# Sliding-window attention and a gated feed-forward network on one core: part of the start-up order, the third half's transposes and the last output block are arranged anew

## The chip, the core and the metric

The kernel runs on one core of a Trainium2 chip. The metric is the device time of one execution in microseconds (us). Times of the kernel before are the median of seven runs; a profile is taken of one further execution.

The engines have the profile's names: PE is TensorE (matmul; PEld its weight load), DVE is VectorE, ACT is ScalarE, POOL is GpSimd, SP is SyncE. Each runs its own instructions in the order in which the program gives them and waits for others by semaphores. DMA transfers are issued by SyncE or by GpSimd.

## The reference

```
# q, k, v: (4, 8, 768, 64) float32; n_global = 8, n_local = 96
scores = q @ k^T / 8
keep   = key is one of the first 8 tokens, or 0 <= query - key < 96
dist   = |query - key|, or 96 where a global key is not local
scores = where(keep, scores - slope[h] * dist, -1e9)      # slope[h] = 2^-(h+1)
a      = softmax(scores)
x      = (a @ v), heads put side by side: (3072, 512)
out    = (relu(x @ w_gate) * (x @ w_val)) @ w_out         # 512 -> 1536 -> 512
```

The output is 3072x512 float32.

## The kernel before, in words

**Tiles.** The 3072 queries are taken in eight *halves* of 384 (half s is batch s//2, part s%2 of its 768 tokens), the heads in four *pairs* p. Keys are grouped in seven tiles of 120 local keys and the 8 global ones (128 partitions). For a half and pair, `piece_t(s, p)` (L280) transposes q and k on TensorE into one PSUM bank; `piece_copy` (L294) brings them to SBUF on VectorE: the keys by `put_keys` (L259) in three copies (L270, L271, and L272, a small copy from kT to kT that spreads the global keys), the queries in two (L300), into qT, where each head of a pair has the other's rows at zero (`zero_q`, L194, sets those zeros with two memsets). Half 0 is loaded as float32 in four parts of two heads by SyncE and cast on chip by `piece_cast` (L250), so one transpose takes both heads of a pair (six per pair). Halves 1 and 2 are cast by the load itself (`load_qk_cast`, L117, four transfers on GpSimd's queue) and need one transpose of 64 columns per head (twelve per pair). Halves 3 to 7 are loaded by SyncE, cast by GpSimd (L338, L346) and transposed by DMA.

**Scores.** For half 0 and pairs 0, 1 and 3 of half 1 the distance bias is put into PSUM by matmuls (`piece_bias`, L304, from `sid` and `dd`), then `piece_biased` (L316) adds the products of q and k (L330) in three groups of one bank and takes the exponential of each (L335). Everywhere else `piece_qk` takes the product (L382), the exponential (L385) and multiplies with a mask `m_all[h]` on VectorE (L394). `setup_mask(h)` (L237) makes the eight masks on ScalarE.

**Values and norm.** `piece_av_wide` (L430) makes the denominators (keys' ones) and the value sums of a pair in two banks (L441); `piece_norm_wide` (L448) takes Ln (L451) and Exp (L453) on ScalarE and multiplies on VectorE (L456) into xT[half], a slice per pair. Four slices make the input of the feed-forward network.

**Feed-forward.** `ffn_pieces(c)` (L468) gives, for each of 12 column groups fc, `gate` (four matmuls of 384 columns, L478, one for each slice of xT; Relu on ScalarE, L487) and `val` (four more; multiplication with the Relu on VectorE into ht, L494); and for three row blocks n `outp` (twelve matmuls of 512 columns, L501, a copy on ScalarE, L506, one store of 256 KB by SyncE, L507). The weights come in three groups of four fc (`load_w`, L168: wg0, wv0, ... 512 KB each in bf16 after casting). PSUM has eight banks: three "qk", two "av", three "ff".

**Order.** All engines follow the order of the program text. Halves 0 and 1 are interleaved by hand (L553–L655); after them `weave` places attention pieces between feed-forward pieces by their share of the work (f_items are the backbone, placed items stand at a share of its sum). GpSimd's order is, at the start: the constants of the masks (affine_select), v's globals and tiles 0 to 3 (L138, L151), half 1's k, q, k, q of four heads each (L128), wg0, wv0 (L168), zeroing (L198, L592 to L594), v tiles 4 to 6, weight groups 1 and 2, half 2's k and q, wo; then v of half 2, zeroing for batch 1, v of half 3. Half 2's transposes and copies lie at 0.55 to 0.95 of the first `weave`:

```
T2 = [(0.0, f) for p in range(HP) for f in (lambda p=p: piece_t(2, p, *QKB), lambda p=p: piece_copy(2, p))]
weave(f1_1[G[0]] + f1_0[G[1]][4:] + f1_1[G[1]], ..., spread(T2, 0.55, 0.95))
```

F0 is the list of half 0's gate and val pieces: F0[2*fc] is gate(fc), F0[2*fc+1] is val(fc).

Of the kernel before, what the change touches and what calls it, by code (L numbers as in the profile page):

```python
# [15 lines left out]
def kernel(  # L16
# [12 lines left out]
    nc = tc.nc  # L29
# [43 lines left out]
    gr_pool = ctx.enter_context(tc.tile_pool(name="gr", bufs=3))  # L73
# [31 lines left out]
    def load_qk(s, h0, h1):  # L105
        b, half = divmod(s, 2)
        if s not in qs_of:
            qs_of[s] = stage.tile([128, H, NN * D], FP32, name="qs")
            ks_of[s] = stage.tile([128, H, NN * D], FP32, name="ks")
        for src, dst in ((k, ks_of[s]), (q, qs_of[s])):  # L110
            nc.sync.dma_start(
                out=dst[:, h0:h1, :],
                in_=src[b, h0:h1, half * QH : (half + 1) * QH, :].rearrange(
                    "h (p n) d -> p h (n d)", n=NN))
# [3 lines left out]
    def load_qk_cast(s, parts=2):  # L118

        b, half = divmod(s, 2)  # L120
        n = H // parts
        for i, (src, name) in enumerate(((q, "qs"), (k, "ks"))):
            t = stage.tile([128, H, NN * D], FP32, name=name)
            qk16[s, i] = t.rearrange("p h x -> p (h x)").bitcast(BF16).rearrange(
                "p (h x) -> p h x", h=H)[:, :, 0 : NN * D]
        for h in range(0, H, n):
            for i, src in ((1, k), (0, q)):
                nc.gpsimd.dma_start(  # L128
                    out=qk16[s, i][:, h : h + n],
                    in_=src[b, h : h + n, half * QH : (half + 1) * QH, :].rearrange(  # L130
                        "h (p n) d -> p h (n d)", n=NN))
# [55 lines left out]
    gsrc = setupp.tile([NG, 2, NN, WQ], FP32)  # L187
    gl = setupp.tile([NG, 2, NN, WQ], FP32)
# [32 lines left out]
    nc.gpsimd.affine_select(out=gl[:, 0], in_=gsrc[:, 0], compare_op=ALU.is_ge, fill=BIG,  # L221
# [3 lines left out]
    nc.gpsimd.affine_select(out=gl[:, 1], in_=gsrc[:, 1], compare_op=ALU.is_ge, fill=BIG,  # L225
# [91 lines left out]
    def piece_biased(s, p):  # L317
# [6 lines left out]
        for g, bank in enumerate(banks_of_half[half]):  # L324
            ps = qk_of[s, p][g]
            es = es01[:, g] if g < 2 else es2
            c = 0
            for j, a, w, m in bank:
                n_ = 2 * NN * w
                nc.tensor.matmul(ps[:, c : c + n_], lhsT=kt[:, j, :], rhs=qd[:, :, :, a : a + w],  # L330
                                 start=False, stop=True, skip_group_check=True)
# [138 lines left out]
    def ffn_pieces(c):  # L470
# [11 lines left out]
        def gate(fc, d0=0, d1=N_DC):  # L482
            psg = products(f"g{fc % 2}", wg, fc, d0, d1)
# [77 lines left out]
    load_qk_cast(1)  # L561
    load_w_group(0)
    for h in range(2, 6):
        setup_mask(h)
# [3 lines left out]
    cast(0, 1, V, V)  # L568
    cast(0, 2, A, A)
# [4 lines left out]
    piece_biased(0, 0)  # L574
# [24 lines left out]
    load_qk_cast(2)  # L599
# [3 lines left out]
    def S1(p):  # L603
        if p == 2:
            for g in range(3):
# [29 lines left out]
    AV(1, 2, *QKB)  # L635
    F0[7]()
# [5 lines left out]
    for h in (0, 1, 6, 7):  # L642
        setup_mask(h)
    load_v_half(2)
# [8 lines left out]
    T2 = [(0.0, f) for p in range(HP) for f in (lambda p=p: piece_t(2, p, *QKB), lambda p=p: piece_copy(2, p))]  # L653
# [52 lines left out]
```

The softmax here doesn't subtract the row's maximum and nothing guards it: scores larger than these inputs give would overflow.

## Time and profile before

| | |
|---|---|
| median of 7 runs | 253.21 us (253.14 to 253.85) |
| the profiled execution | 252.88 us |
| its span | 251.1 us |
| busy, share of the span | PE 95%, ACT 62%, DVE 55%, POOL 35% |
| TensorE matmuls | 1741, 239.7 us busy |
| feed-forward products (L478) | 768 of 326 ns |
| output products (L501) | 280 recorded, 379 ns busy each |

The span is the time from the first to the last instruction that the profiler shows; the execution's own time has 1.8 us more around it. The page divides the span into 40 slices of 6.3 us each and gives each engine's busy share in tenths. "Idle before <-X" behind a group of instructions says how long its engine stood idle just before them and who released it. A time in microseconds without further words is a point on the span's axis.

### The profile page before, as it was taken

The page shows a single profiled execution, that of the slowest core. Times are in us where ns is not written, and L with a number is a line of the kernel's source. Part 1 is how long each engine was busy: PE and PEld are TensorE (multiplying, and loading weights), DVE is VectorE, ACT ScalarE, POOL GpSimd, SP SyncE. Part 2 cuts the span into 40 slices and gives each one's busy share as a digit, 9 for nine tenths or more (in the row PEclk, how much of TensorE's full clock was granted, in tenths as well). Part 3 has the DMA queues.
Part 4 walks back from the last instruction along what each step waited for, and adds up shares of the span by engine and source line. Part 5 has one row for each costly group of instructions (what it writes and reads, how often), then busy time and mean ns, then how long its engine had stood idle before and what let it go on. Part 6 is the DMA issues. An engine that isn't in the chain of part 4 may idle for free.

```text
span 251.1 us, 4845 instructions
## 1 busy us (share of the span) xinstructions
PE 239.7 (95%) x1741; PEld 142.5 (57%) x1749; DVE 137.3 (55%) x352; ACT 156.8 (62%) x323; POOL 88.5 (35%) x205
## 2 busy tenths in 40 slices
PE   7678999999999999999999999999999999999993
PEld 4565665556445566556664666556655666556541
DVE  5959557966441467527662557527662557424410
ACT  7886774257654687557774687557774687553321
POOL 8997442059491076203627065303520000000000
PEclk9999999999999999999999999999999999999998
DMA  6999999959599667738468958738432100020012
GB/s 183 174 182 189 206 197 207 138 162 140 83 208 160 197 162 162 53 109 265 106 86 89 252 158 158 56 111 261 104 86 82 43 3 0 19 110 0 0 42 84
DMA packets 77431, 31.56 MB, mean 126 GB/s; under 512 B 57440, under 2 KB 74336, under 8 KB 77408
## 3 DMA queue, kind: packets, MB, share of 16 engines
q0 software_dynamic: 36080, 9.48, 37.0%
q1 hardware_dynamic: 41328, 21.78, 32.0%
q8 instruction: 13, 0.21, 0.4%
q14 instruction: 10, 0.08, 0.1%
HBM read 28.38 MB, written 6.29 MB: 138 GB/s over the span
## 4 chain that ended last, share of the span: by engine, by line
PE 83%; DVE 7%; ACT 6%; DMA 1%; issue 1%; SPq 1%; ACTq 0%
PE ff_ps L478 45%; PE ff_ps L501 24%; PE av_ps L410 5%; PE qk_ps L382 5%; DVE xT L427 2%; DMA qs<-in_q_dram 1%; DVE ht L494 1%; ACT es L335 1%; PE av_ps L441 1%; ACT grelu L487 1%; ACT rcp L424 1%; PE qk_ps L330 1%; ACT lnd L419 1%; DVE qT L300 1%; PE qk_ps L290 1%
## 5 line engine op out<-in xcount | busy, mean ns | idle before, releaser
L478 PE MATMUL ff_ps<-xT,wv 128*128 128x384 bf16 x384 | 78.1, 326 | 0.8 <-DVE ht L494 0.3
L478 PE MATMUL ff_ps<-xT,wg 128*128 128x384 bf16 x384 | 78.1, 326 | 0.0
L487 ACT ACTIVATE grelu<-ff_ps 128x384 bf16<-128x384 f32 x96 | 46.9, 489 | 33.7 <-DVE ht L494 12.5
L501 PE MATMUL ff_ps<-wo_sb,ht 128*128 128x512 bf16 x280 | 66.4, 379 | 0.4
L494 DVE TENSOR_TENSOR ht<-ff_ps,grelu 128x384 bf16<-128x384 f32 x96 | 53.3, 555 | 21.3 <-PE ff_ps L478 13.3
L427 DVE TENSOR_TENSOR xT<-av_ps,rcp 64x384 bf16<-64x384 f32 x48 | 26.7, 555 | 46.2 <-ACT rcp L424 41.6
L478 PEld LDWEIGHTS <-wv 128*128 128x128 bf16 x384 | 36.0, 97 | 23.4 <-issue 2.1
L478 PEld LDWEIGHTS <-wg 128*128 128x128 bf16 x384 | 36.0, 97 | 22.9
L394 DVE TENSOR_TENSOR es<-es,m_all 128x432 bf16<-128x432 bf16 (+5 forms) x113 | 34.4, 333 | 26.1 <-ACT es L385 25.3
L385 ACT ACTIVATE es<-qk_ps 128x432 bf16<-128x432 f32 (+2 forms) x75 | 39.4, 529 | 9.4 <-PE qk_ps L382 7.7
L501 PEld LDWEIGHTS <-ht 128*128 128x128 bf16 x288 | 27.0, 97 | 28.3
L419 ACT ACTIVATE lnd<-av_ps 64x384 f32<-64x384 f32 x48 | 23.3, 485 | 13.3 <-PE av_ps L410 12.6
L506 ACT COPY osb<-ff_ps 128x512 f32<-128x512 f32 x24 | 14.0, 585 | 26.7 <-PE ff_ps L501 25.9
L338 POOL CAST kc<-ks 128x384 bf16<-128x384 f32 x20 | 10.1, 550 | 51.7 <-DMA ks<-in_k_dram 51.7
L382 PE MATMUL qk_ps<-qT,kT 128*128 128x432 bf16 (+5 forms) x113 | 25.8, 286 | 0.0
L151 POOL DMA_DIRECT2D vbuf<-in_v_dram x28 | 24.3, 874 | 4.0 <-DMA wg<-in_moe_w_gate_dram 2.4
L410 PEld LDWEIGHTS <-vbuf 128*128 128x128 bf16 x216 | 18.3, 98 | 8.6 <-issue 0.8
L410 PE MATMUL av_ps<-es,vbuf 128*128 128x216 bf16 (+4 forms) x216 | 21.4, 226 | 0.6 <-DVE xT L427 0.6
L382 PEld LDWEIGHTS <-kT 128*128 128x128 bf16 x113 | 10.9, 98 | 7.5
L424 ACT ACTIVATE rcp<-lnd 128x384 f32<-128x384 f32 x24 | 12.5, 523 | 0.8
L346 POOL CAST qz<-qs 128x192 bf16<-128x192 f32 x40 | 12.2, 353 | 1.4 <-DMA qs<-in_q_dram 1.4
L335 ACT ACTIVATE es<-qk_ps 128x432 bf16<-128x432 f32 (+2 forms) x15 | 7.0, 536 | 3.4 <-PE qk_ps L330 3.3
(92 smaller groups left out, 146.1 us busy)
## 6 DMA issues: line engine op xcount, KB each, us to landing
out_dram<-osb SPq DMA_DIRECT2D x24, 256.0 KB
ks<-in_k_dram SPq DMA_DIRECT2D x5, 768.0 KB
qs<-in_q_dram SPq DMA_DIRECT2D x5, 768.0 KB
vbuf<-in_v_dram POOLq DMA_DIRECT2D x24, 120.0 KB, 4.6
wg<-in_moe_w_gate_dram POOLq DMA_DIRECT2D x3, 512.0 KB, 8.8
wv<-in_moe_w_val_dram POOLq DMA_DIRECT2D x3, 512.0 KB, 10.5
wo_sb<-in_moe_w_out_dram POOLq DMA_DIRECT2D x1, 1536.0 KB, 19.0
ks<-in_k_dram SPq DMA_DIRECT2D x4, 192.0 KB
```

Of the source, the lines that this page charges most:

```text
L151: nc.gpsimd.dma_start(out=v_dst(b, NG + r0, NG + r0 + n, j), in_=v[b, :, KT * j + r0 : KT * j + r0 + n, :].rearrange("h p d -> p h d"))
L382: nc.tensor.matmul(ps[:, c : c + n_], lhsT=kt[:, j, :], rhs=qd[:, :, :, a : a + w], start=True, stop=True)
L385: nc.scalar.activation(es[:, 0:cols], ps[:, 0:cols], AF.Exp, bias=0.0, scale=scale)
L394: nc.vector.tensor_mul(e4, e4, mk)
L410: nc.tensor.matmul(av3[:, :, a : a + w], lhsT=vb[:, j, z0 : z0 + 128], rhs=es[:, c : c + NN * w].rearrange("k (n p) -> k n p", n=NN), star ...
L419: nc.scalar.activation(ln[o0 : o0 + 64], av[d0 : d0 + 64, 0:QH], AF.Ln, bias=0.0, scale=1.0)
L424: nc.scalar.activation(rc, ln, AF.Exp, bias=0.0, scale=-1.0)
L427: nc.vector.tensor_tensor(xT_of[s][r, p, :], av_of[s, p, e_][r, 0:QH], rc[r], op=ALU.mult)
L478: nc.tensor.matmul(st[key][:, 0:QH], lhsT=w_of(w, dc, fc), rhs=xT_of[c][:, dc, :], start=(dc == 0), stop=(dc == N_DC - 1))
L487: nc.scalar.activation(gr, psg[:, 0:QH], AF.Relu, bias=0.0, scale=1.0)
L494: nc.vector.tensor_tensor(ht[:, fc, :], psv[:, 0:QH], st["r", fc], op=ALU.mult)
L501: nc.tensor.matmul(ps2, lhsT=ht[:, fc, n * 128 : (n + 1) * 128], rhs=wo_sb[:, fc, :], start=(fc == 0), stop=(fc == N_FC - 1))
```

## The change

- Half 1's q and k: four transfers as before, but wg0 is issued between the first two and the last two (so wg0 comes earlier in the queue, the last two later).
- Of the masks, only number 4 is made at the start; 5 is made ahead of the scores of half 1's pair 2, and 0, 1, 2, 3, 6, 7 behind F0[11].
- Half 0's cast of pair 1 goes from VectorE to ScalarE; pair 2's q cast is put between the first and second exponential of pair 0's scores (`between`).
- Half 1's first transposes, and their copies, are put among half 0's last scores and norms: t(1,0) ahead of the scores of pair 3, copy(1,0), t(1,1) and copy(1,1) around the second norm. `zero_q` for half 1 now stands behind these copies in the program; the two write the same tile.
- Gates 0 to 2 of half 0 take three of their four slices first, and the last one after the scores of half 1's pair 0. The order of what follows is new too. Four Relu buffers instead of three.
- Half 2's q and k are loaded as float32 (768 KB each, on GpSimd's queue), cast by GpSimd in pairs, and transposed in six transposes a pair; transposes and copies of a pair are one item of `weave`. The loads of v for half 2 stand behind these casts.
- The last block of rows of the last half is computed and stored in columns 0–255, 256–383 and 384–511, the last copied by VectorE.
- Two constants of the masks' set-up are bf16, one of them half as large.

```diff
@@ -105 +105 @@
-    def load_qk(s, h0, h1):
+    def load_qk(s, h0, h1, eng=nc.sync):
...
-    def load_qk_cast(s, parts=2):
...
+    def load_qk_cast(s, h0=0, h1=H):
...
@@ -283,10 +281,10 @@
-                for e in range(1 if s == 0 else 2):
-                    r = slice(0, 128) if s == 0 else slice(64 * e, 64 * e + 64)
-                    src = (cast_of[s, p][:, i, n] if s == 0
-                           else qk16[s, i][:, 2 * p + e, n * D : (n + 1) * D])
+                for e in range(2 if s == 1 else 1):
+                    r = slice(64 * e, 64 * e + 64) if s == 1 else slice(0, 128)
+                    src = (qk16[s, i][:, 2 * p + e, n * D : (n + 1) * D] if s == 1
+                           else cast_of[s, p][:, i, n])
@@ -317 +315 @@
-    def piece_biased(s, p):
+    def piece_biased(s, p, between=None):
@@ -335 +333 @@
+            if g == 0 and between is not None:
+                between()
@@ -482 +482 @@
-            psg = products(f"g{fc % 2}", wg, fc, d0, d1)
+            psg = products(f"g{fc % 4}", wg, fc, d0, d1)
@@ -510,8 +510,24 @@
         for fc in range(N_FC):
             f1.append((0.65, lambda *d, fc=fc: gate(fc, *d)))
             f1.append((0.65, lambda *d, fc=fc: val(fc, *d)))
+        def outp_cols(n, c0, c1, copy):
+            ps2 = ff_psum.tile([128, 512], FP32, name="ff_ps")
+            for fc in range(N_FC):
+                nc.tensor.matmul(ps2[:, 0 : c1 - c0], lhsT=ht[:, fc, n * 128 : (n + 1) * 128],
+                                 rhs=wo_sb[:, fc, c0:c1], start=(fc == 0), stop=(fc == N_FC - 1))
+            if c0 == 0:
+                st["osb"] = osb_pool.tile([128, DM], FP32, name="osb")
+            osb = st["osb"]
+            copy(osb[:, c0:c1], ps2[:, 0 : c1 - c0])
+            nc.sync.dma_start(out=out_v[c, n][:, c0:c1], in_=osb[:, c0:c1])
+
         f2 = []
         for n in range(NN):
+            if c == NHALF - 1 and n == NN - 1:
+                f2.append((1.3, lambda n=n: outp_cols(n, 0, 256, nc.scalar.copy)))
+                f2.append((0.7, lambda n=n: outp_cols(n, 256, 384, nc.scalar.copy)))
+                f2.append((0.7, lambda n=n: outp_cols(n, 384, 512, nc.vector.tensor_copy)))
+                continue
             for part in range(2):
                 f2.append((1.3, lambda n=n, part=part: outp(n, part)))
         return f1, f2
@@ -558,34 +574,39 @@
     load_v_globals(0)
     for j in range(4):
         load_v(0, j)
-    load_qk_cast(1)
-    load_w_group(0)
-    for h in range(2, 6):
-        setup_mask(h)
+    load_qk_cast(1, 0, H // 2)
+    load_w(wg[0], moe_w_gate, 0, GW * 128)
+    load_qk_cast(1, H // 2, H)
+    load_w(wv[0], moe_w_val, 0, GW * 128)
+    setup_mask(4)
     warm_up(7)
     piece_bias(0, 0)
     cast(0, 0, V, V)
-    cast(0, 1, V, V)
-    cast(0, 2, A, A)
+    cast(0, 1, A, A)
+    piece_cast(0, 2, 1, A)
     piece_t(0, 0)
     piece_copy(0, 0)
     piece_bias(0, 1)
     piece_t(0, 1)
-    piece_biased(0, 0)
+    piece_biased(0, 0, lambda: piece_cast(0, 2, 0, A))
     piece_copy(0, 1)
     piece_t(0, 2)
     piece_biased(0, 1)
     piece_copy(0, 2)
     cast(0, 3, V, V)
-    copy_v_globals(V, 0, 1, 4)
     piece_bias(0, 2)
     piece_biased(0, 2)
     piece_t(0, 3)
+    copy_v_globals(V, 0, 1, 4)
+    piece_bias(0, 3)
     piece_copy(0, 3)
-    piece_bias(0, 3)
     AV(0, 0)
+    piece_t(1, 0, *QKB)
     piece_biased(0, 3)
+    piece_copy(1, 0)
     AV(0, 1)
+    piece_t(1, 1, *QKB)
+    piece_copy(1, 1)
 
     zero_q(P, 1)
     for p in range(HP):
@@ -596,52 +617,55 @@
         load_v(0, j)
     load_w_group(1)
     load_w_group(2)
-    load_qk_cast(2)
+    load_qk(2, 0, H, nc.gpsimd)
     load_w(wo_sb, moe_w_out, 0, DM)
 
 
     def S1(p):
         if p == 2:
+            setup_mask(5)
             for g in range(3):
                 piece_qk(1, p, g)
         else:
             piece_bias(1, p)
             piece_biased(1, p)
 
-    piece_t(1, 0, *QKB)
-    AV(0, 2, *QKB)
-    piece_copy(1, 0)
-    piece_t(1, 1, *FFB)
+    def TC(s, p, *pool):
+        piece_t(s, p, *pool)
+        piece_copy(s, p)
+
+    gate, val = F0[0:8:2], F0[1:8:2]
+    AV(0, 2, *FFB)
     AV(0, 3)
-    piece_copy(1, 1)
+    gate[0](0, LAST)
     S1(0)
+    for f in gate[1:3]:
+        f(0, LAST)
+    for f in gate[0:3]:
+        f(LAST, N_DC)
     copy_v_globals(V, 0, 4, NT)
-    piece_t(1, 2, *FFB)
+    S1(1)
+    piece_t(1, 2)
+    piece_t(1, 3)
     piece_copy(1, 2)
-    S1(1)
-    piece_t(1, 3, *FFB)
     piece_copy(1, 3)
-    F0[0]()
+    gate[3]()
     S1(2)
-    F0[1]()
-    F0[2]()
+    val[0]()
+    val[1]()
     AV(1, 0)
-    F0[3]()
     S1(3)
-    F0[4]()
-    F0[5]()
+    val[2]()
     AV(1, 1)
-    F0[6]()
+    val[3]()
     AV(1, 2, *QKB)
-    F0[7]()
     F0[8]()
     AV(1, 3)
     F0[9]()
     F0[10]()
     F0[11]()
-    for h in (0, 1, 6, 7):
+    for h in (0, 1, 2, 3, 6, 7):
         setup_mask(h)
-    load_v_half(2)
     for p in range(HP):
         nc.gpsimd.memset(kT[1][p][:, 3, 32:128].bitcast(mybir.dt.uint32), 0)
         nc.gpsimd.memset(kT[1][p][:, 6, NG + 48 : 128].bitcast(mybir.dt.uint32), 0)
@@ -650,7 +674,10 @@
         nc.gpsimd.memset(qz[i].rearrange("t n p e z -> t (n p e z)").bitcast(mybir.dt.uint32), 0)
     for j in range(NT):
         fill_ones(nc.gpsimd, 1, j)
-    T2 = [(0.0, f) for p in range(HP) for f in (lambda p=p: piece_t(2, p, *QKB), lambda p=p: piece_copy(2, p))]
+    for p in range(HP):
+        cast(2, p, P, P)
+    load_v_half(2)
+    T2 = [(0.0, lambda p=p: TC(2, p, *QKB)) for p in range(HP)]
     weave(f1_1[G[0]] + f1_0[G[1]][4:] + f1_1[G[1]],
           [(0.05 + 0.06 * j, lambda j=j: fill_ones(nc.vector, 0, j)) for j in range(NT)],
           [(0.6, lambda: load_qk_after(3)), (0.6, lambda: load_v_half(3))],
```

More of the change, by code (lines that the diff above doesn't have):

```diff
@@ L72 @@
     ht_pool = ctx.enter_context(tc.tile_pool(name="ht", bufs=2))
-    gr_pool = ctx.enter_context(tc.tile_pool(name="gr", bufs=3))
+    gr_pool = ctx.enter_context(tc.tile_pool(name="gr", bufs=4))
     osb_pool = ctx.enter_context(tc.tile_pool(name="osb", bufs=2))
@@ L110, in load_qk @@
         for src, dst in ((k, ks_of[s]), (q, qs_of[s])):
-            nc.sync.dma_start(
+            eng.dma_start(
                 out=dst[:, h0:h1, :],
@@ L116 @@
     qk16 = {}
-    def load_qk_cast(s, parts=2):
+    def load_qk_cast(s, h0=0, h1=H):
         b, half = divmod(s, 2)
[L121 to L131, printed above, removed]
+        for i, src, name in ((1, k, "ks"), (0, q, "qs")):
+            if (s, i) not in qk16:
+                t = stage.tile([128, H, NN * D], FP32, name=name)
+                qk16[s, i] = t.rearrange("p h x -> p (h x)").bitcast(BF16).rearrange(
+                    "p (h x) -> p h x", h=H)[:, :, 0 : NN * D]
+            nc.gpsimd.dma_start(
+                out=qk16[s, i][:, h0:h1],
+                in_=src[b, h0:h1, half * QH : (half + 1) * QH, :].rearrange(
+                    "h (p n) d -> p h (n d)", n=NN))
     def v_dst(b, r0, r1, j):
@@ L186 @@
         load_qk(0, 2 * p, 2 * p + 2)
-    gsrc = setupp.tile([NG, 2, NN, WQ], FP32)
-    gl = setupp.tile([NG, 2, NN, WQ], FP32)
+    gsrc = setupp.tile([NG, NN, WQ], BF16)
+    gl = setupp.tile([NG, 2, NN, WQ], BF16)
     warm = setupp.tile([128, 128], BF16)
@@ L220 @@
     q1, q2 = [[1, NN], [NN, WQ]], [[0, 2], [-1, NN], [-NN, WQ]]
-    nc.gpsimd.affine_select(out=gl[:, 0], in_=gsrc[:, 0], compare_op=ALU.is_ge, fill=BIG,
+    nc.gpsimd.affine_select(out=gl[:, 0], in_=gsrc, compare_op=ALU.is_ge, fill=BIG,
                             base=-NL, pattern=q1, channel_multiplier=-1)
@@ L224 @@
                             base=0, pattern=q1, channel_multiplier=-1)
-    nc.gpsimd.affine_select(out=gl[:, 1], in_=gsrc[:, 1], compare_op=ALU.is_ge, fill=BIG,
+    nc.gpsimd.affine_select(out=gl[:, 1], in_=gsrc, compare_op=ALU.is_ge, fill=BIG,
                             base=-(NL - 1), pattern=q1, channel_multiplier=0)
```

## The prediction, as put on record before the changed kernel was run

> **What bounds the kernel now.** I read the page's busy line, slices and chain first.
>
> ```profile
> PE 239.7 (95%) x1741; PEld 142.5 (57%) x1749; DVE 137.3 (55%) x352; ACT 156.8 (62%) x323; POOL 88.5 (35%) x205
> ...
> PE   7678999999999999999999999999999999999993
> ...
> PE 83%; DVE 7%; ACT 6%; DMA 1%; issue 1%; SPq 1%; ACTq 0%
> ```
>
> TensorE bounds it: only the first four slices (25 us) and the last have gaps. Windows of the stages that the change touches (columns: sum, then busy time of PE, PEld, DVE, ACT, POOL; clock; DMA share; GB/s):
>
> ```profile
> 13.90:22.90 9.00, 7.49 (x137) 5.76 (x134) 6.29 (x20) 6.44 (x15) 7.92 (x15) 1.00 1.47 186
> 22.90:35.90 13.00, 13.00 (x151) 8.33 (x150) 7.67 (x20) 10.20 (x23) 5.91 (x8) 1.00 1.35 202
> 44.10:52.00 7.90, 7.90 (x85) 4.70 (x85) 7.55 (x27) 1.96 (x4) 0.00 (x0) 1.00 1.29 108
> ```
>
> From 22.9 us TensorE is full; whatever is to be won in front of it is idle time before that. Between 44 and 52 VectorE is nearly full too (7.55 of 7.90) and GpSimd idle. Full speed of the clock (1.00) throughout. The page's own time was 252.88 (span 251.1 and 1.8 around it); the median of seven runs is 253.21, 0.33 above. I add up against 252.88 and put 0.33 on top.
>
> **1. Up to 13.9 us: 0.** Moving the cast (0,1) from VectorE to ScalarE would let the first copy of half 0 start at about 5.8 instead of 6.39. It gains nothing, by the timelines of VectorE and GpSimd:
>
> ```profile
> 6.94 0.26 DVE L272 COPY kT<-kT 128x56 bf16<-128x56 bf16 x1
> ...
> 8.34 0.64 DVE L272 COPY kT<-kT 128x56 bf16<-128x56 bf16 x1
> ...
> 9.98 0.54 DVE L272 COPY kT<-kT 128x56 bf16<-128x56 bf16 x1
> ```
>
> ```profile
> 5.36 3.62 POOL L151 DMA_DIRECT2D vbuf<-in_v_dram  x4
> 8.96 0.80 POOL L128 DMA_DIRECT2D ks<-in_k_dram  x1
> ```
>
> The small SBUF-to-SBUF copy L272 takes 0.18 when GpSimd is quiet (45.32, 47.19, 49.05, 50.92). Here it ends, within 7 ns each time, where an issue of GpSimd ends (7.20, 8.98, 10.52): it waits for the issue in progress. A copy 0.6 earlier comes just behind the issue end at 6.29 and ends at 7.20 again. The bf16 selections on GpSimd: 0; the affine_selects lie on one line by element count whatever their type (216 elements 0.36–0.53, 432 0.58–0.60). Bounds −0.9 (everything one issue of GpSimd earlier) to +0.1.
>
> **2. 13.9 to 35.9: +0.97.** Half 1's k and q of pairs 0 and 1 (cast on load, GpSimd's queue) land at 13.69 and 14.73 in before (q issued 9.73, 5.0 to landing), and stand at the same place in the queue in the changed kernel. Now t(1,0) stands in TensorE's order ahead of qk(0,3), which ran at 14.00, and both wait for q:
>
> ```profile
> 14.00 0.68 PE L330 MATMUL ff_ps<-qT,kT 128*128 128x432 bf16 x4
> ...
> 17.27 0.45 PE L441 MATMUL av_ps<-es,vbuf 128*64 128x216 bf16 x8 [0.42 <-DVE xT L456]
> ...
> 18.20 0.37 PE L312 MATMUL qk_ps<-dd,sid 128*128 128x192 bf16 x4 [0.17 <-DVE xT L456]
> 19.45 0.34 PE L312 MATMUL qk_ps<-dd,sid 128*128 128x216 bf16 x2 [0.87 <-DVE qT L300]
> 19.63 0.75 PE L330 MATMUL qk_ps<-qT,kT 128*128 128x144 bf16 x5
> ```
>
> The columns are start, time, engine, line, operation, and in brackets the idle time before it and its releaser. So qk(0,3) starts at 14.73 and 0.33 (six transposes of q)≈15.08, 1.08 late. Behind it, row by row:
>
> - ScalarE: its exponentials (1.29 for three) end 16.77; then ln and exp of pairs 1, 2, 3 in a chain (0.43+0.50 each): 17.71, 18.63, 19.57.
> - VectorE, in its new order: xT01 (0.56) to 18.30; copy(1,1) to 19.54 (1.32, the sum of L270–L300 without a held L272); xT02 to 20.12; xT03 to 20.60.
> - The partial gate products take three of four k-slices, xT00–02. TensorE reaches them at 18.74; two slices run, the third waits for 20.12. So they cover 0.3 of a gap of 1.4, since copy(1,1) stands before xT02.
> - GpSimd: the zeroing of half 1's qT (L198, 2×0.73), which ran at 13.53, now waits by the changed program's dependences for copy(1,1), 19.54; it ends 21.13. qk(1,0) waits for it: 21.18 instead of 19.63. Behind it in GpSimd's in-order queue: kT and vbuf zeroing, v tiles 4–6, weight groups 1 and 2, k and q of half 2, wo, then the casts.
> - TensorE from there (bias 0.6, qk 0.6, transposes 0.33 and 0.12 for the switch, product 0.65, values 0.28 each): rest of gates 0–2 to 23.24; bias and qk(1,1) 24.44; t(1,2), t(1,3) 25.32; gate 3 25.97; copy(1,2) ends 26.42, so 0.5 of stall, and qk(1,2) starts 26.47; values 0 and 1 of the FFN 28.46; qk(1,3) 30.41; value 3 32.65; last three products to 36.84. Before, the same product F0[11] ended at 35.87.
>
> So +0.97: TensorE's work is the same, and about 3.6 us instead of 2.4 are idle before it is dense. Late loads hold nothing by their rows (issue to landing 8.8 and 10.5 for a weight tile): v 4–6 about 27.9 (needed 28.8), group 1 30.5 and 33.0 (needed 33.4, 34.9). Bounds −0.1 (the partial gates cover all and q lands by 13.9) to +1.5 (v tiles 0.5 later than worked out).
>
> **3. Masks: +0.90.** Of eight exponentials of the bias masks four ran early and four here; now one is early, one ahead of pair 2, and six are here, on ScalarE between two relus:
>
> ```profile
> 35.42 0.49 ACT L487 ACTIVATE grelu<-ff_ps 128x384 bf16<-128x384 f32 x1 [0.67 <-PE ff_ps L478]
> 35.81 1.91 ACT L237 ACTIVATE m_all<-dd 128x432 bf16<-128x432 bf16 x4
> 37.62 0.89 ACT L487 ACTIVATE grelu<-ff_ps 128x384 bf16<-128x384 f32 x2
> ```
>
> ```profile
> 38.15 0.81 PE L478 MATMUL ff_ps<-xT,wv 128*128 128x384 bf16 x4 [0.17 <-ACT grelu L487]
> ```
>
> Four already hold TensorE 0.33 (37.82 to 38.15; three FFN banks are all it may run ahead). Two more, 2×0.453 by their spacing, come wholly on top: no cover is left. Bounds +0.4 (if ScalarE stands a product further ahead) to +0.9.
>
> **4. Half 2's transposes: −0.12.** Twelve half-width transposes per pair cost TensorE 0.55 with their two switches; six full-width ones of casts by GpSimd 0.33: 4×0.22=−0.88. But VectorE had a period of 1.86 there (1.36 copy and 0.5 ht) for 1.86 of TensorE, so TensorE, now at 1.63, waits for it; and GpSimd's issues of v for half 2, queued behind the casts, fall at about 47–54, where it was idle, and hold L272 of pairs 1–3 by 0.2–0.6 (step 1's rows): stalls of about 0.76. Bounds −0.88 to +0.7. k and q, 768 KB each as fp32, land about 40 and 42.4 at the rate of SyncE's load of the same shape (325–365 GB/s), so q's first cast ends at about 43 against a need at 45.87; at the casting queue's 206 GB/s, 45.4, which adds 0.2–0.5. GpSimd's casts: 0.55 each (row L338). The Trainium skill ("SBUF — State Buffer", Who interferes with whom) says that VectorE in its two-port modes and GpSimd lock a shared port pair for a whole instruction. L272 agrees. For this step it would have L272 wait for a running cast of GpSimd as well; by the page, as an estimate, one cast of 0.55 more, 254.6 in all, against 254.05 by the rows; no row of before has L272 beside such a cast.
>
> **5. Last block in columns: −0.9.** After the last product (ends 247.10):
>
> ```profile
> 247.19 0.58 ACT L506 COPY osb<-ff_ps 128x512 f32<-128x512 f32 x1 [2.05 <-PE ff_ps L501]
> ```
>
> Copy to 247.77, SyncE's issue to 248.13, data 248.63–249.44 (0.815 for 256 KB), end 251.1. A 128-column copy on VectorE takes about 0.28 (0.17 for 24, 0.56 for 384): −0.3; the last 64 KB a quarter of 0.815: −0.6. The products are the same (columns add up). Bounds −0.3 (transfer time fixed) to −1.2.
>
> **Sum:** 0+0.97+0.90−0.12−0.90=**+0.85**; 252.88+0.85+0.33≈**254.05**.
>
> **Rivals.** About 0.2% (0.5 us) is what measurement tells from no change. (a) Forecast, 253.75–254.6: chance 0.45. (b) The second half's stages are not held: GpSimd's issues of v end before copy(2,1) or lie between the copies; place the four pairs near 46–52, price the 0.76; +0.09, 253.3, not slower. It decides if fewer than half the L272 there exceed 0.2. For it: four issues of 0.8 in 7.4 us miss some copies; against: all four small copies in the early rows were held. 0.16. (c) k/q of half 2 or casts late, or copies held by casts: +0.6 to +1.3, 254.6–255.3. For: everything on GpSimd's queue starts 6 us later; against: 3 us margin by SyncE's rate. 0.17. (d) The reorder works: q lands by 13.9 or the gates cover the front; term 2 goes to 0, 253.1: 0.12; with (b), 252.3: 0.05. (e) The change doesn't do what it says: the partial gates wait as whole ones (xT03's time), +0.3 more, 254.35: 0.05.
>
> Faster (below 252.7): the joint case 0.05, and with the low bounds of steps 1 and 5 0.05 of (d) and 0.02 of (b): 0.12. Same: 0.14 of (b), 0.07 of (d), 0.04 of (a): 0.25. Slower: 0.41 of (a), (c), (e): 0.63. The range reaches from (b) and (d) at low bounds to (c)'s upper part, 252.6 to 255.2, and leaves out the joint case and (c)'s end.
>
> **What would show it.** Step 2: qk(0,3) at about 15.1, a wait of qk(1,0) for POOL near 21, F0[11] ending about 36.8. Step 3: six masks in a row and a TensorE gap of about 1.2 behind them. Step 4: six transposes a pair, L272 above 0.2 and ending with GpSimd's issues. Step 5: a last copy of 0.28 and about 0.9 less from last product to end. Wrong if qk(0,3) still starts by 14.1, or if masks leave no gap.

## The result, and the profile after

The changed kernel took 254.70 us (median of 14 runs, 253.82 to 255.37) against 253.22 for the kernel before on the same occasions (33 runs): ratio 1.0050, 95% interval 1.0038 to 1.0061. It is slower by about 1.3 to 1.5 us. The forecast was 254.05, range 252.6 to 255.2. The profiled execution took 254.82, its span is 252.8 (before: 252.88 and 251.1).

In what follows t(s,p), copy(s,p) and qk(s,p) are the transposes, the copies and the scores of half s's pair p, and wg1 and wv1 the gate and value weights of the second weight group.

The page after, the same three lines as of before:

```profile
PE 239.1 (95%) x1741; PEld 143.7 (57%) x1749; DVE 134.8 (53%) x351; ACT 157.5 (62%) x326; POOL 91.0 (36%) x211
...
PE   7768988999999999999999999999999999999995
...
PE 75%; DMA 7%; ACT 6%; POOL 4%; DVE 4%; issue 2%; POOLq 0%; ACTq 0%; DVEq 0%
```

TensorE has the same work. But the chain that ended last now runs 7% through DMA (before 1%) and 4% through GpSimd (before none): the start of the program waits for loads. The windows say the same (same columns as before; the second now ends where F0[11] ends, 38.12 instead of 35.87, and the third is half 2's transposes, 3 us later; the columns are sum, then busy time of PE, PEld, DVE, ACT, POOL; clock; DMA share; GB/s):

```profile
13.90:22.90 9.00, 6.65 (x101) 4.77 (x102) 5.40 (x15) 5.25 (x12) 3.07 (x9) 1.00 1.16 168
22.90:38.12 15.22, 13.86 (x179) 8.98 (x178) 8.60 (x24) 11.49 (x26) 13.91 (x28) 1.00 1.10 143
47.10:55.00 7.90, 7.90 (x67) 5.25 (x64) 7.40 (x27) 2.50 (x6) 7.90 (x12) 1.00 1.49 167
```

GpSimd was busy 7.92 in the first window and is now busy 3.07; its work has moved into the second window (13.91 of 15.22). TensorE idles 2.35 in the first window (1.51 before) and 1.36 in the second (0.00 before).

Where the time went is read best by one clock: the start of the n-th feed-forward matmul of 384 columns (L478; four of them make one gate or value product). Each kernel has 768 of these matmuls, all recorded, counted here from 0. Their order is the same in both kernels from the 32nd on.

| matmul | before | after | difference |
|---|---|---|---|
| 0 (first gate slice) | 22.87 | 18.83 | −4.04 |
| 32 (fifth gate) | 32.42 | 33.67 | +1.25 |
| 48 (behind F0[11]) | 35.87 | 38.12 | +2.25 |
| 60 (behind the masks) | 38.15 | 41.30 | +3.15 |
| 92 (ahead of half 2's transposes) | 43.35 | 46.50 | +3.15 |
| 150 (behind them) | 55.54 | 57.79 | +2.25 |
| last product of TensorE ends | 247.10 | 249.69 | +2.59 |
| span ends | 251.1 | 252.8 | +1.7 |

So the front costs 2.25, the masks 0.90, half 2 gives 0.90 back, and the last block 0.88 (from the last product's end to the span's end 4.01 before, 3.13 after). The other 0.34 come in bit by bit between 58 and 247. Of them 0.28 lie ahead of the last feed-forward product, where e4 below, whose program is that of before up to there, shows 0.27 too; so this isn't the change. The remaining 0.06 are in the last block's own products.

TensorE's timeline after, the rows that answer to those shown of before:

```profile
14.89 0.36 PE L288 MATMUL qk_ps<-ident,qs 128*64 128x128 bf16 x6 [0.67 <-DMA qs<-in_q_dram]
15.18 0.69 PE L328 MATMUL ff_ps<-qT,kT 128*128 128x432 bf16 x4
...
20.26 0.32 PE L478 MATMUL ff_ps<-xT,wg 128*128 128x384 bf16 x1 [0.93 <-DVE xT L456]
...
21.25 0.75 PE L328 MATMUL qk_ps<-qT,kT 128*128 128x144 bf16 x5
...
36.16 0.82 PE L478 MATMUL ff_ps<-xT,wv 128*128 128x384 bf16 x4 [0.93 <-DMA wv<-in_moe_w_val_dram]
...
41.30 0.81 PE L478 MATMUL ff_ps<-xT,wv 128*128 128x384 bf16 x4 [1.06 <-ACT grelu L487]
```

Row 1: TensorE waits for q's landing. Row 2: half 0's last scores, at 14.00 before. Row 3: the third slice of the partial gate waits 0.93 for xT02. Row 4: half 1's first scores, at 19.63 before. Row 5: wv1 lands late. Row 6: the masks, which stand in a row on ScalarE:

```profile
38.06 2.81 ACT L235 ACTIVATE m_all<-dd 128x432 bf16<-128x432 bf16 x6
```

GpSimd's timeline has the cause of row 5. Before:

```profile
13.53 1.52 POOL L198 MEMSET qT<- 64x768 uint32 x2
...
18.93 0.80 POOL L168 DMA_DIRECT2D wg<-in_moe_w_gate_dram  x1
```

After:

```profile
12.85 0.78 POOL L166 DMA_DIRECT2D wv<-in_moe_w_val_dram  x1
19.68 1.52 POOL L196 MEMSET qT<- 64x768 uint32 x2 [6.05 <-DVE qT L298]
...
25.30 0.80 POOL L166 DMA_DIRECT2D wg<-in_moe_w_gate_dram  x1
```

The zeroing waits 6.05 us for VectorE's copy, and all later work of GpSimd waits behind it, the loads of v and of the weight groups 1 and 2 among it.

In half 2, two pairs' transposes on TensorE, before (first the keys' six of twelve) and after (six in all):

```profile
44.09 0.36 PE L290 MATMUL qk_ps<-ident,ks 128*64 128x128 bf16 x6
...
45.95 0.36 PE L290 MATMUL qk_ps<-ident,ks 128*64 128x128 bf16 x6
```

```profile
47.15 0.50 PE L288 MATMUL qk_ps<-ident,qk 128*128 128x128 bf16 x6
...
48.78 0.50 PE L288 MATMUL qk_ps<-ident,qk 128*128 128x128 bf16 x6
```

The pairs follow one another at 1.63 instead of 1.86.

### The profile page after: what moved, and what is told of

Its sections match the earlier page's. It is cut to its first block, busy times and chain, and to the rows that moved or that the text cites. A ratio compares the mean times of both kernels' runs of the same rounds, so it can differ in the third digit from the quotient of the medians.

```text
span 252.8 us, 4857 instructions
## 1 busy us (share of the span) xinstructions
PE 239.1 (95%) x1741; PEld 143.7 (57%) x1749; DVE 134.8 (53%) x351; ACT 157.5 (62%) x326; POOL 91.0 (36%) x211
## 4 chain that ended last, share of the span: by engine, by line
PE 75%; DMA 7%; ACT 6%; POOL 4%; DVE 4%; issue 2%; POOLq 0%; ACTq 0%; DVEq 0%
PE ff_ps L478 41%; PE ff_ps L501 23%; PE av_ps L410 5%; PE qk_ps L382 4%; DMA wv<-in_moe_w_val_dram 4%; DVE xT L427 2%; DMA qs<-in_q_dram 2%; POOL vbuf L149 1%; ACT grelu L487 1%; DMA vbuf<-in_v_dram 1%; ACT rcp L424 1%; ACT lnd L419 1%; DVE ht L494 1%; PE ff_ps L516 1%; ACT m_all L235 1%
## 5 line engine op out<-in xcount | busy, mean ns | idle before, releaser
L478 PE MATMUL ff_ps<-xT,wv 128*128 128x384 bf16 x384 | 77.9, 326 | 2.8 <-ACT grelu L487 1.1
L478 PE MATMUL ff_ps<-xT,wg 128*128 128x384 bf16 x384 | 78.1, 326 | 1.0 <-DVE xT L456 0.9
L501 PE MATMUL ff_ps<-wo_sb,ht 128*128 128x512 bf16 x268 | 63.8, 379 | 0.4
L478 PEld LDWEIGHTS <-wv 128*128 128x128 bf16 x384 | 36.1, 97 | 25.5 <-issue 3.3
L478 PEld LDWEIGHTS <-wg 128*128 128x128 bf16 x384 | 36.1, 97 | 22.7 <-DMA wg<-in_moe_w_gate_dram 0.3
L394 DVE TENSOR_TENSOR es<-es,m_all 128x432 bf16<-128x432 bf16 (+5 forms) x113 | 32.4, 316 | 25.9 <-ACT es L385 25.3
L501 PEld LDWEIGHTS <-ht 128*128 128x128 bf16 x276 | 25.8, 97 | 26.9
L506 ACT COPY osb<-ff_ps 128x512 f32<-128x512 f32 x23 | 13.5, 585 | 24.7 <-PE ff_ps L501 23.8
L382 PE MATMUL qk_ps<-qT,kT 128*128 128x432 bf16 (+5 forms) x113 | 25.8, 286 | 0.3 <-DVE qT L298 0.3
L382 PEld LDWEIGHTS <-kT 128*128 128x128 bf16 x113 | 10.9, 98 | 8.0 <-DVE qT L298 0.7
L333 ACT ACTIVATE es<-qk_ps 128x432 bf16<-128x432 f32 (+2 forms) x15 | 7.1, 538 | 2.5 <-PE qk_ps L328 2.4
```

What stands on the lines that cost most here:

```text
L394: nc.vector.tensor_mul(e4, e4, mk)
L478: nc.tensor.matmul(st[key][:, 0:QH], lhsT=w_of(w, dc, fc), rhs=xT_of[c][:, dc, :], start=(dc == 0), stop=(dc == N_DC - 1))
L501: nc.tensor.matmul(ps2, lhsT=ht[:, fc, n * 128 : (n + 1) * 128], rhs=wo_sb[:, fc, :], start=(fc == 0), stop=(fc == N_FC - 1))
```

## The experiments

All kernels were timed against the kernel before on the same chip. Up to the exponential of `piece_biased` (L335, L333 after) line numbers after are two below those of before (the small copy L272 is L270 after); those of L382 to L506 are the same.

A profile shows one execution. The span of every execution is on record as well, and the profiled one can lie at either end:

| kernel | executions | span of the profiled one | spans, median (range) |
|---|---|---|---|
| changed | 14 | 252.8 | 252.75 (252.0–253.3) |
| e1 | 12 | 252.8 | 252.35 (251.3–253.9) |
| e2 | 12 | 251.5 | 252.15 (251.5–253.6) |
| e3 | 6 | 254.7 | 255.3 (254.5–256.4) |
| e4 | 12 | 250.6 | 250.7 (250.4–251.5) |
| before, beside e1–e4 | 29 | | 251.3 (251.1–253.5) |
| e5 | 12 | 251.0 | 251.6 (250.6–252.9) |
| e6 | 12 | 250.9 | 251.3 (250.7–252.1) |
| e7 | 12 | 250.8 | 249.95 (249.5–250.8) |
| e8 | 10 | 249.8 | 250.0 (249.6–250.6) |
| before, beside e5–e8 | 33 | | 251.5 (251.2–252.7) |
| e9 (the changed kernel) | 10 | 253.5 | 253.1 (251.9–253.7) |
| e10 | 9 | 249.6 | 250.2 (249.5–251.1) |
| e11 | 6 | 249.8 | 250.0 (249.3–250.3) |
| before, beside e9–e11 | 18 | | 251.6 (251.2–252.6) |
| e12 | 10 | 249.6 | 249.95 (249.5–251.6) |
| before, beside e12 | 14 | | 251.55 (251.1–252.4) |

**e1: the zeroing ahead of the copies.**

```diff
     load_w(wv[0], moe_w_val, 0, GW * 128)
+    zero_q(P, 1)
     setup_mask(4)
...
     piece_copy(1, 1)
-    zero_q(P, 1)
```

> The changed kernel with the zeroing of half 1's query tile put back ahead of the first copy into it, so that GpSimd's queue behind it no longer waits for VectorE. Theory (the wait holds GpSimd's queue 6.05 us, and the second weight group comes late): weight tiles wg1 and wv1 land at about 28 and 30.5 instead of 33.62 and 36.12, the stalls of 0.27 and 0.97 in front of their products go, qk(1,0) starts about 0.25 earlier; F0[11] ends near 36.6 instead of 38.1, and the whole is 1.3 to 1.6 us shorter, about 253.2. Rival (the new order itself, t(1,0) ahead of qk(0,3), costs nearly all of the 2.25 and the loads only fill its gaps): at most 0.3 us shorter, 254.4 or more.

254.30 us, ratio 1.0033 (1.0009 to 1.0058): 0.4 less than the changed kernel, as by the medians of the spans: short of the theory, near the rival. The trace says more. wv1 lands at 31.08 and nothing waits for it. But half 1's q landed at 15.68 in this execution, 0.83 later than in the changed kernel's, and the first gate slice started at 19.67, 0.84 later; F0[11] ended 0.56 earlier nevertheless. From q's landing on, the zeroing gave 1.39, as the theory had it, and in this execution the landing took 0.83 away. When q landed in the other eleven isn't recorded, so that this explains their median isn't shown. Hence e5 and e9.

**e2: the six late masks one at a time between the Relus of the next products.**

```diff
-    for h in (0, 1, 2, 3, 6, 7):
-        setup_mask(h)
...
+          [(0.04 + 0.08 * i, lambda h=h: setup_mask(h)) for i, h in enumerate((0, 1, 2, 3, 6, 7))],
```

> The changed kernel with the six late masks made one at a time between the Relus of the following feed-forward products instead of in a row. Theory (six in a row hold the next Relu, and TensorE waits 1.23): the gap of 1.23 goes without a new one, 1.1 to 1.25 us shorter, about 253.5. Rival (ScalarE has no room there either, each mask delays a Relu that TensorE waits for): gaps of 0.1 to 0.2 per mask come back, at most 0.4 shorter.

254.21 us, ratio 1.0038 (1.0017 to 1.0059); span 251.5, 1.3 less than the changed kernel's. ScalarE's timeline shows masks and Relus in turn:

```profile
38.06 0.49 ACT L487 ACTIVATE grelu<-ff_ps 128x384 bf16<-128x384 f32 x1 [0.81 <-PE ff_ps L478]
38.45 0.56 ACT L235 ACTIVATE m_all<-dd 128x432 bf16<-128x432 bf16 x1
39.36 0.49 ACT L487 ACTIVATE grelu<-ff_ps 128x384 bf16<-128x384 f32 x1 [0.36 <-PE ff_ps L478]
39.74 1.01 ACT L235 ACTIVATE m_all<-dd 128x432 bf16<-128x432 bf16 x2
```

No gap is left: from matmul 56 to 60 this kernel gains 0.33 on before, where the changed one loses 0.90, so 1.23 in all. Two things blur the time. wv1 happened to land 0.92 earlier here (35.20 instead of 36.12), so part of the front's loss is chance; and 0.44 is lost again at half 2's transposes, which now wait for its q (landed 44.99): the rival named for e6. The profiled execution is the shortest of the twelve. The medians are 0.5 (time) and 0.6 (span) under the changed kernel's, not far from the 0.79 that 1.23 less 0.44 leave. So the gap is worth what the theory said, but the time doesn't gain as much.

**e3: half 2 loaded, cast and transposed as before, in the changed kernel.**

```diff
-    load_qk(2, 0, H, nc.gpsimd)
+    load_qk_cast(2, 0, H // 2)
+    load_qk_cast(2, H // 2, H)
...
-    for p in range(HP):
-        cast(2, p, P, P)
-    load_v_half(2)
```

(piece_t takes twelve transposes for it again, and v is issued ahead of the zeroing of batch 1's tiles.)

> The changed kernel with half 2 loaded, cast and transposed as before (cast on load, twelve transposes a pair, v issued ahead). Theory (the six transposes save TensorE 0.22 a pair and VectorE's lag is made up by the banks): about 0.9 us longer, 255.6. Rival (the step as it was forecast: VectorE's period and held copies take the saving away): 0.0 to 0.2 longer.

257.15 us, ratio 1.0158 (1.0122 to 1.0194): 2.45 more than the changed kernel. Half 2's stage alone gives what the theory says: matmul 92 to 150 costs as much as before (this kernel is 2.37 behind before at both), 0.90 more than in the changed kernel. Another 1.63, between matmuls 150 and 200, were expected by neither theory. The waits of GpSimd in this kernel, 44 to 60 us, hold one row (us in total, times, longest):

```profile
POOL vbuf L674 <- DMA vbuf<-vbuf: 13.8, 1, 13.8
```

The zeroing of batch 1's v tile waits until v's globals, behind wo in the late queue, have landed and been spread; half 3's casts come 2.3 us late, and TensorE waits for half 3's keys at 76.72. So, by this trace, the changed place of v's loads, behind the zeroing, is itself worth 1.63 as long as the queue is late; it wasn't run by itself.

**e4: the last block in columns, alone, in the kernel before** (the hunk with outp_cols).

> The kernel before with the last block in columns and nothing else. Theory (last copy 0.3 shorter, last store a quarter of the data): 0.9 us shorter, about 252.3. Rival (the end is set by a store's fixed time, whatever its size): only the 0.3 of the copy, 252.9.

252.51 us, ratio 0.9963 (0.9943 to 0.9982): −0.7 by the medians, −0.6 by those of the spans. From the last product's end to the span's end 3.21, against 4.01. Its last copy, on VectorE:

```profile
247.47 0.29 DVE L521 COPY osb<-ff_ps 128x128 f32<-128x128 f32 x1 [7.26 <-PE ff_ps L516]
```

0.29 instead of 0.58 for the copy; and from the copy's end to the span's end, with a store of 64 instead of 256 KB, 2.83 instead of 3.34. So the rival (only the copy's 0.3) fails, and the theory holds by the stage, 0.80 of 0.9; the medians say a little less.

**e5: half 1's first transposes behind the scores of half 0's pair 3 again, nothing else.**

```diff
     AV(0, 0)
-    piece_t(1, 0, *QKB)
     piece_biased(0, 3)
+    piece_t(1, 0, *QKB)
     piece_copy(1, 0)
```

> The changed kernel with one piece moved: half 1's first transposes stand behind the scores of half 0's pair 3 again, so that these scores do not wait for q's landing. Theory (TensorE is pinned to the landing of half 1's q by this one piece, and all behind it follows): qk(0,3) starts near 13.5 instead of 15.2, the norms, copy(1,1), the zeroing and the second weight group all come 1.2 to 1.5 us earlier, F0[11] ends near 36.7 instead of 38.1, the whole about 253.3; and the time scatters less than that of the changed kernel (253.8 to 255.4), since q's landing differs by up to 0.95 between executions. Rival (the landing only moves to the transposes themselves, and the queue of GpSimd sets the end): at most 0.4 shorter, 254.3.

253.50 us, ratio 1.0007 (0.9986 to 1.0028): 1.1 less than the changed kernel by the ratios, 1.4 less than e9, which is the changed kernel on the same chip; all from the move of twelve transposes. q landed at 15.10 here, and TensorE did other work until then:

```profile
14.04 0.68 PE L328 MATMUL ff_ps<-qT,kT 128*128 128x432 bf16 x4
14.65 0.36 PE L288 MATMUL qk_ps<-ident,ks 128*64 128x128 bf16 x6
15.15 0.36 PE L288 MATMUL qk_ps<-ident,qs 128*64 128x128 bf16 x6
```

F0[11] ends at 36.26 instead of 38.12, 0.4 better than expected; wv1 landed 1.86 earlier, of which the earlier issue explains only 0.94. The first gate slice now waits 0.90 for wg0, the first gate weights (landed 18.81). The masks' gap is there unchanged. The second half of the expectation failed: the times scatter as widely (252.5 to 255.1). By the time the theory holds.

**e6: the zeroing and the masks together** (the edits of e1 and e2).

> The changed kernel with the zeroing ahead of the copies and with the six masks spread among the Relus. Theory (the two costs are apart and add): against the changed kernel -0.6 to -1.4 for the first, as q lands, and -1.2 for the second; 252.1 to 252.9. Rival (what is gained in front is lost again at half 2's transposes, which wait for its q at about 45): at least 0.5 of it comes back, 253.0 or more.

253.45 us, ratio 1.0005 (0.9990 to 1.0019). By the time the rival holds. F0[11] ends at 36.74, 0.87 behind before, with q landing at 14.86 and no late weights. The rival is right in that something is lost at half 2, but it isn't q (landed at 40.29): VectorE's small copies are held. VectorE's timeline:

```profile
45.86 0.30 DVE L270 COPY kT<-kT 128x56 bf16<-128x56 bf16 x1
...
47.86 0.18 DVE L270 COPY kT<-kT 128x56 bf16<-128x56 bf16 x1
...
49.73 0.62 DVE L270 COPY kT<-kT 128x56 bf16<-128x56 bf16 x1
...
51.81 0.32 DVE L270 COPY kT<-kT 128x56 bf16<-128x56 bf16 x1
```

The three long ones end at 46.17, 50.35 and 52.13; a cast of GpSimd ended at 46.14 and issues at 50.34 and 52.13. Half 2 gives 0.60 instead of 0.90. In the changed kernel the same four take 0.23, 0.24, 0.18 and 0.18.

**e7: e6 and e5 together.**

> The changed kernel with all three: zeroing ahead, masks spread, half 1's first transposes behind the scores of pair 3. Theory: the front is then as fast as before's or faster (0 to -0.5), the masks' gap of 0.33 goes too, half 2 gives 0.9 and the last block 0.7: 250.8 to 251.5. Rival (half 2's q, which lands at about 45, is now needed at about 43.5): 0.5 to 1.0 of it is lost there, 251.8 to 252.3.

252.15 us, ratio 0.9948 (0.9930 to 0.9966): within the rival's range, though half 2's q (landed 41.44) held nothing. The profiled execution is the longest of the twelve, with q landing at 16.03. In it the front is 0.86 behind before's (F0[11] at 36.73), and the third slice of gate 0 waits 0.93 for xT02. e6 ends F0[11] at 36.74 with q landing 1.17 earlier; so, if the landing is allowed for, the move of the transposes is worth about that, and the medians of the spans are 1.35 apart (0.95 when only those executions of e6 count whose granted clock was 0.998 or more). Against before the median span is 1.55 shorter. Masks (0.33), half 2 (0.60) and last block (0.8 to 0.9) add up to 1.7 to 1.8, which leaves 0.2 to 0.3 that the front still costs: an estimate. So the theory's front, as fast as before's, is missed by that much, and by 0.86 in the profiled execution.

**e8: the kernel before with its own front, and three parts**: last block, half 2 (load, casts, six transposes, v behind the casts), its four late masks spread.

> The kernel before with its front as it was, and with three parts: the last block in columns, half 2 loaded as fp32 and transposed in six (casts on GpSimd, v issued behind them), and its four late masks spread among the Relus. Theory (each part is worth what its stage shows: -0.7, -0.9, -0.33): 251.2 to 251.5. Rival (half 2's q needs a full transfer of 768 KB on GpSimd's queue and lands later than the cast one, and the transposes wait): 251.7 to 252.3.

251.98 us, ratio 0.9944 (0.9927 to 0.9961), in the rival's range; −0.78 at matmul 150, +0.14 in the front. q of half 1 landed at 15.68 here, 0.95 later than in the profile of before, and the whole front is 0.14 behind: the old order takes a late q almost without loss. Half 2's q landed at 40.72, before it was needed, so the rival's reason fails; half 2 gives 0.60 as in e6, with the same held copies.

**e9: the changed kernel once more.**

> The changed kernel itself, unaltered, beside the other runs on one chip. Theory: half 0's first gate product starts 3.98 after the landing of half 1's q, whatever that is here (14.8 to 16), and the whole follows it one to one; 254.3 to 255.0. Rival (the front's loss is fixed work and the landing is coincidence): gate 0 starts at 18.8 again.

255.36 us, ratio 1.0062 (1.0038 to 1.0086), 0.4 above the range of the theory. TensorE's timeline:

```profile
15.34 0.36 PE L288 MATMUL qk_ps<-ident,qs 128*64 128x128 bf16 x6 [1.32 <-DMA qs<-in_q_dram]
...
19.28 0.50 PE L478 MATMUL ff_ps<-xT,wg 128*128 128x384 bf16 x2
```

q landed at 15.29, gate 0 started at 19.28, 3.99 later. The five profiles in which t(1,0) stands ahead of the scores and the zeroing or the masks vary (the changed kernel twice, e1, e2, e3) have landings of 14.83 to 15.68 and distances of 3.98, 3.99, 3.99, 3.98 and 3.99; e6, where both vary, has 4.06. The start of gate 0 follows the landing one to one, as the theory has it. F0[11] ends at 38.62 here: wg1 and wv1 landed at 34.00 and 36.61.

**e10: e7, with t(1,1) and copy(1,1) behind the partial gate products.**

```diff
     piece_copy(1, 0)
     AV(0, 1)
-    piece_t(1, 1, *QKB)
-    piece_copy(1, 1)
...
     for f in gate[1:3]:
         f(0, LAST)
+    piece_t(1, 1)
+    piece_copy(1, 1)
```

(Then follow the last slices of gates 0 to 2, t(1,2), copy(1,2), gate 3, the scores of pair 1, t(1,3), the copy of v's globals and copy(1,3).)

> The kernel with all three undone (zeroing ahead, masks spread, first transposes behind pair 3's scores), and with the transposes and copies of half 1's pair 1 moved behind the partial gate products; the copy of v's globals stands behind the copy of pair 2. Theory (VectorE's copy of pair 1 stands between two norms and holds xT02, for which the third slice of gate 0 waits 0.9): that wait falls to 0.1 or so, and F0[11] ends 1.0 to 1.4 earlier than with the three undone, 250.8 to 251.2. Rival (the wait turns up at the scores of pair 1, whose copies are now later): 0.3 or less is won, 251.8.

252.56 us, ratio 0.9953 (0.9934 to 0.9972), as the rival has it (little is won), though not where it put the loss. In the profile F0[11] ends 0.86 earlier than in e7, at 35.87 like before's; xT02's wait is gone, and the last norm's value product now waits 1.34 for ScalarE, at 18.04. But q landed at 14.93 here and at 16.03 in e7, and the profiled executions are the second shortest of nine and the longest of twelve. The medians of the spans are 250.2 and 249.95. So that the copy between the norms cost 0.86 isn't shown, and by the time the move wins nothing.

**e11: e8 with half 2's small copies on ScalarE.**

```diff
-            copy_small(kt[:, :, 0:NG], kt[:, 0:1, NG : 2 * NG].to_broadcast([128, NT, NG]))
+            (copy_g or copy_small)(kt[:, :, 0:NG], kt[:, 0:1, NG : 2 * NG].to_broadcast([128, NT, NG]))
...
+                 nc.scalar.copy if s == 2 else None)
```

> The kernel before with its three parts (last block, half 2, masks spread), and in half 2's four pairs the small SBUF-to-SBUF copy on ScalarE instead of VectorE. Theory (this copy waits for the running issue or cast of GpSimd, 0.12 to 0.45 a pair, and VectorE's lag then holds TensorE 0.3 behind the pairs): the 0.3 goes, 251.7 against 251.98. Rival (the hold costs nothing, the lag is VectorE's own period): 0.0 to 0.1, or longer by what ScalarE's Relus wait.

251.86 us, ratio 0.9925 (0.9904 to 0.9946). The copy takes 0.24 on ScalarE in all four pairs. The first runs beside a cast, begun 0.23 into it, where VectorE's in e8 was held (0.30); the others begin 0.80 to 0.91 into an issue, just ahead of its end, so they say nothing about issues:

```profile
45.22 0.24 ACT L272 COPY kT<-kT 128x56 bf16<-128x56 bf16 x1 [1.28 <-DVE kT L270]
```

From matmul 92 to 130 this kernel gains 0.91 on before, e8 0.60. That could also be VectorE's shorter period with a copy less; but the changed kernel and e9, whose four copies on VectorE were hardly held, take 7.52 there, this kernel 7.51, and the five kernels with held copies (e1, e6, e7, e8, e10) 7.82 to 7.83. So the hold cost 0.3, as the theory had it; the medians (0.1 apart in time, none in span) are too close to show it.

**e12: all of it, with half 0's second norm ahead of t(1,0).**

> All of it together: the kernel of e10 (zeroing ahead, masks spread, both transposes of half 1's pairs 0 and 1 later, last block in columns, half 2 as changed), half 2's small copies on ScalarE as in e11, and half 0's second norm ahead of half 1's first transposes, so that no norm waits for q's landing. Theory: against e10 the front gives 0.3 to 0.65 more (ScalarE's chain of norms starts at 15.0 instead of 15.6) and half 2 gives 0.3; the span 248.7 to 249.0 and the time 250.6 to 251.5. Rival (another wait takes the place of the norms', or ScalarE's Relus wait for the small copies): 251.9 or more.

251.85 us, ratio 0.9938 (0.9917 to 0.9958), just under the rival's 251.9; median span 249.95, like e7's: what was won in one place is lost in another. The value products no longer wait 1.34 for ScalarE (0.70 for VectorE is left, at 17.11), and the first gate slice (L479 in this kernel) now waits for weights:

```profile
18.20 0.50 PE L479 MATMUL ff_ps<-xT,wg 128*128 128x384 bf16 x2 [0.64 <-DMA wg<-in_moe_w_gate_dram]
```

F0[11] ends at 36.04, 0.17 behind before's. The best kernels here (e7, e8, e10, e11, e12) have intervals that overlap, 0.47 to 0.75% below before; their median spans are 1.4 to 1.6 us shorter than those of before beside them.

## Why the prediction was right, step by step

The forecast of +0.85 met +1.48 (medians) and +1.9 (the two profiled executions). The sign was right, and the time lies in the range. But it lies above the forecast's own part of it (253.75 to 254.6), in that of rival (c), whose reason held nothing here; and that it lies in the range owes something to luck: one term came out 1.28 too small, beyond its bound of +1.5, and another 0.78 too large, and the two cancelled in part.

- **Step 1, 0.** The sum was right, the reason half wrong. The copies were not held at the same boundaries: those at 6.42 and 8.09 took 0.18. Half 0's first values ran 0.6 earlier (13.00 instead of 13.61), and the wait for q's landing took it back.
- **Step 2, +0.97, measured +2.25.** Its order of events came out within 0.15 (forecast in brackets): qk(0,3) at 15.18 (15.08), copy(1,1) done at 19.6 (19.54), the third slice at 20.26 (20.12), qk(1,0) at 21.25 (21.18), qk(1,2) at 26.55 (26.47), value 3 ending 32.7 (32.65). What failed is the sentence that late loads hold nothing: wg1 and wv1 landed at 33.62 and 36.12 instead of 30.5 and 33.0 and cost 0.27 and 0.93, which with the 0.97 make 2.17 of the 2.25. The prediction named a row for it, 8.8 and 10.5 from issue to landing, and did not use it: issued at 25.30 and 26.06, they would land by it at 34.1 and 36.6, too late. Instead it put each about 2.5 behind what came before. Even before's wg1 took 3.3 behind the last v tile (24.43 to 27.74), and here it took 5.2 (28.43 to 33.62). Wherever the zeroing held the queue, so that little was left in it, wg1 took 3.7 to 5.2 behind v (the changed kernel 5.2, e9 5.1, e2 and e5 4.0, e3 3.7); elsewhere 2.5 to 3.7. From 28.5 to 33.5 the changed kernel's DMA moved 165 GB/s, e2's 186; before's, from 24.5 to 29.5, 207. So the front's price differs from execution to execution: 2.25 here, 2.75 in e9, 1.33 and 1.47 in e2 and e3, where wg1 and wv1 landed near 32.5 and 35.2. Why the rate differs stays open.
- **Step 3, +0.90, measured +0.90.** Spread out in e2, the masks leave no gap, and before's own 0.33 is gone too.
- **Step 4, −0.12, measured −0.90**, all that TensorE saves (−0.88, the low bound). VectorE's period of 1.87 was as forecast; its lag behind TensorE's 1.63 is made up in the products after the pairs, so it costs nothing by itself. The hold of the small copy exists, but its price was sized at 0.76: in the changed kernel it was 0.1 of holding and no stall, and in e6 to e8 0.7 of holding and 0.3 of stall. The loads of half 2's k and q took 2.42 and 2.23 from the landing before to their own (325 and 353 GB/s), as forecast, but began behind the late weights. The lock that the Trainium skill describes ("SBUF — State Buffer", Who interferes with whom) also holds the copy behind a cast, as the page says and as no row of before showed: e6's first copy ended 0.03 after the cast. For GpSimd's issues the rows don't bear out a hold for the whole instruction (see the last section).
- **Step 5, −0.90, measured −0.88** (e4: −0.80).

Of the rivals, (b) is what half 2 did, at a price within 0.1 of the one given, but the front's late weights hid it. Its own sign, fewer than half of the small copies above 0.2, is on the line (0.23, 0.24, 0.18, 0.18). (c) did not occur: q of half 2 landed at 45.85, when the front was itself late enough; in e2, with the masks spread, it held 0.44. (d) fails: no profiled execution had q by 13.9 (14.73 to 16.03). (e) did not occur: the partial products ran two slices ahead and then waited for xT02, as step 2 had it, not for xT03.

## What to carry to other kernels

Before an instruction is moved so that an engine's queue waits on another engine, count what stands behind it in that queue, DMA issues above all, and carry the landing times on from the rows of issue to landing, with a margin for a queue that was held and has little left in it (here 3.7 to 5.2 us for the next weight tile instead of 2.5 to 3.7). A piece that waits for a load, put ahead of work that doesn't, makes what stands behind it follow that load's landing one to one (3.98 to 4.06 behind it in six profiles); put behind that work, the same load was 0.95 late for at most 0.14 (e8). Work of an engine off the bound, such as the masks, is best given out singly between the instructions that the bound waits for; and a small copy that GpSimd's casts hold on one engine may fit on another (0.30 on VectorE, 0.24 on ScalarE). One profile is one execution: before a microsecond is read from a pair of profiles, see where each stands among its kernel's spans.

## What the runs showed of the hardware that was not expected

- Whether a copy is held depends on when it begins. With an issue of GpSimd running, copies begun 0.09 and 0.21 us into it took 0.18 (the changed kernel at 6.42, e6 at 47.86); those begun 0.25 to 0.6 into it nearly all ended with it (before at 8.34 and 9.98, e6 at 49.73). Two did not and took 0.18: one of e4, begun 0.26 into an issue (at 8.54), and one of e2, 0.43 into a short one (at 48.63). Casts of GpSimd held copies begun 0.16 to 0.23 into them as well (e2 at 46.56, e6 at 45.86). In the changed kernel's half 2 the last three copies begin 0.72 to 0.83 into an issue, close to its end: two issues take 1.8 there and VectorE's period is 1.87, so each copy falls near an end again, and little is held.
- The landing of the same transfer behind the same queue differed from execution to execution: half 1's q 14.73 to 16.03, issued within 0.25 of one another.
- The time of an execution was 1.7 to 2.3 us above its span in most executions and 2.3 to 3.6 in others, with the same program among both: in 4 of 10 of e9 and none of 14 of the changed kernel, and in 11 of the 94 of the kernel before beside the experiments. Nothing that the traces show accounts for it.
- Executions with a lower mean granted clock had longer spans: in e1 four of 0.986 to 0.993 had a median of 253.15 and the other eight 251.85, in e2 four of 0.987 to 0.993 had 253.3 and the others 251.95. None of the experiments' profiles is of such an execution, so where in the span this lies, and which is the cause of which, is open.
